# A convolution and a gated product: five convolution blocks a unit become three, and six blocks for four are made on ScalarE and GpSimd

## The chip, the cores and the metric

The kernel runs on one core of one Trainium2 chip. Its engines work side by side, each on its own queue of instructions: TensorE (PE; its weight loads are shown as PEld), VectorE (DVE), ScalarE (ACT), GpSimd (POOL) and SyncE (SP), which here only issues transfers and waits. The metric is the device time of one execution in microseconds. Before the change the median of three runs is 704.99 us (704.97 to 705.65).

## The reference

Two stages. First a causal depthwise convolution along the sequence, with seven taps a head that are a softmax over the head's weights. Then a two-layer product with the function h cos(h) between the layers.

```python
B, S, D = 8, 4096, 192;  H, K = 8, 7;  Dff = 2048      # group = D // H = 24 channels share a head's taps
w = softmax(weight, axis=-1)                            # weight is [H, K]
x_pad = zeros of K - 1 rows ahead of each sequence
y[b, s, h, g] = sum over k of w[h, k] * x_pad[b, s + k, h, g]
y = y.reshape(B * S, D)                                 # 32768 tokens of 192
hh = y @ moe_w_in                                       # 192 -> 2048
out = (hh * cos(hh)) @ moe_w_out                        # 2048 -> 192, float32
```

## The kernel before

The 32768 tokens are cut into 32 units of 1024 (`U`), and each unit into two tiles of 512 (`T`); a "first" and a "second" tile is meant by that. The 192 channels are three groups `k` of 64, so that a product over the channels is three accumulating steps (`NC`).

For each tile TensorE computes eight h groups (`mm1`, L488): one group is 256 of the 2048 hidden rows, as two halves of 128 by 512 tokens, each with 64 rows of the array, six matmuls in all, into one of three PSUM buffers. ScalarE takes the cosine of a group as a sine with a shifted phase (L510), and VectorE multiplies it with h into `g` (L514). The product with `moe_w_out` (`mm2_step`, L523) runs for the tile before: 64 steps a tile, each a pair of matmuls on the two row halves, 192 columns wide, into two banks. When a tile's 64 steps are done ("p"), the two banks are copied out (`evac`, L567), bank 0 by ScalarE (order letter `P`) and bank 1 by VectorE (`Q`), and stored (`store`).

The convolution reaches the first product as `cT`, channels on the partitions and tokens along the row, twice: once on the lower 64 partitions and once, shifted by one block, on the upper 64. From unit 4 on (`FIRST_RAW`) it is computed in two ways, and a unit is split between them:

- The first `NPB` = 5 blocks of `OP` = 112 tokens go over TensorE. GpSimd casts x to bf16 in the order of channels (`cast_unit`, L207, order letter `K`); `conv_unit` (L269, letters `c1`, `c2`) multiplies with a banded matrix of the taps, in two pieces of four matmul pairs, 16 matmuls a unit; ScalarE copies the result to `ct_buf` (L294, `ec1`, `ec2`); two DMA transposes bring it to `cT` (`turn_unit`, L309, letters `X` and `x`).
- The last `NRB` = 4 blocks of `OR` = 116 tokens stay off TensorE. One DMA transpose turns the cast x ("raw") into `rT`, channels on the partitions (`turn_raw`, L343, letter `T`). ScalarE multiplies three of the seven taps (`taps`, L352, L356; six instructions of half the width each, letters such as `a211`), GpSimd multiplies the other four in one instruction (L363) and sums up (L370, L374, L377; `conv_raw`, letter `R`), and four DMAs write the result `ro` into `cT` (`spread_raw`, L379, L387; letter `U`).

x is loaded three DMAs a unit (`load_unit`, L98, letter `L`).

Every engine's order is written out by hand. `PE_ORDER` and `ACT_ORDER` (L589, L590) have one string for the first and one for the second tile: `h0` to `h7` are the h groups, `m12` is twelve steps of mm2, a letter with a number (`K+3`) is the work above for the unit that lies so many units ahead, `O` a store. `ACT_ORDER` gives the order in which cosines (`s0` to `s7`, with VectorE's product behind each), taps and evacuations are issued. SyncE's queue takes transfers in the order in which TensorE's string names them. It also carries marks: in the middle of each tile (`q`), and between the two convolution pieces, SyncE waits for TensorE's last matmul on one set of row halves, and TensorE waits for SyncE before it writes the same bank from the other halves (class `Turn`, L191).

## Time and profile before

| | |
|---|---|
| median of the runs | 704.99 us (704.97 to 705.65) |
| span of the profiled execution | 703.5 us |
| the profiled execution's own time beside its span | not listed; the median lies 1.5 us over the span |
| TensorE busy | 697.0 us, 99% |
| VectorE busy | 642.4 us, 91% |
| ScalarE busy | 644.4 us, 92% |
| GpSimd busy | 503.7 us, 72% |
| DMA engines | mean 142 GB/s |
| granted TensorE clock | 0.999 |

The span is the time from the first to the last instruction of one execution on the profiler. In a list of groups, a row has the source line, the engine, the operation, what is written and read, the shape, the count, and then the busy time in us, the mean of one in ns, and the idle time of the engine just before these instructions with what ended it. A row of the chain of work is a start and a duration in us and what the end of the program hung on in that time. A row of windows has, for one stretch, the busy time of PE, PEld, DVE, ACT and POOL (with counts), then the clock, the busy share of the DMA engines and GB/s. A row of waits has the waiting instruction, whom it waited for, us in total, the number of times and the longest. A row of the timeline has start, duration, engine, line, operation and count; equal neighbours are merged, so that the first start and the whole duration stand there. SPq is SyncE's queue: the duration is that of the issuing, and the landing of a transfer is counted from the start of its issue.

### The profile page before, as it was taken

To read this page: it belongs to the slowest core of one execution; us is meant where nothing else is said; L and a number is where in the kernel's file an instruction comes from. 1 tells how busy PE (TensorE), PEld (TensorE's weight loads), DVE (VectorE), ACT (ScalarE), POOL (GpSimd) and SP (SyncE) were. 2 spreads that over 40 slices of the span, in tenths; PEclk is the share of its full clock that TensorE was granted. 3 is DMA by queue.
4 is the path that set the end of the run, shared out by engine and by line. 5 is a ranking of instruction groups with operands and counts; after the bars stand their busy time and mean duration, and the time that the engine had idled before them with its cause. 6 is when DMAs were issued, how large, how long until landed. Compare 5 with 4: busy or idle time off the path is not lost.

```text
span 703.5 us, 26826 instructions
## 1 busy us (share of the span) xinstructions
PE 697.0 (99%) x11830; PEld 512.8 (73%) x11830; DVE 642.4 (91%) x598; ACT 644.4 (92%) x831; POOL 503.7 (72%) x214
## 2 busy tenths in 40 slices
PE   8999999999999999999999999999999999999997
PEld 4677777777777777777777777777777777777776
DVE  6889999999999999999999999999999999999996
ACT  7889999999999999999999999999999999999875
POOL 6524478977778877778877688877789778799400
PEclk9999999999999999999999999999999999999999
DMA  8964456667667768676656577577665576874331
GB/s 214 234 167 97 120 135 143 138 147 164 138 153 146 131 145 176 134 152 131 147 152 153 150 159 129 140 161 150 143 147 132 145 174 137 153 127 95 92 91 47
DMA packets 228292, 100.09 MB, mean 142 GB/s; under 512 B 156240, under 2 KB 227792, under 8 KB 228176
## 3 DMA queue, kind: packets, MB, share of 16 engines
q1 hardware_dynamic: 227464, 97.40, 62.7%
q8 instruction: 92, 1.51, 0.9%
q0 software_dynamic: 416, 0.79, 0.7%
q14 instruction: 24, 0.20, 0.1%
q10 hardware_dynamic: 296, 0.20, 0.1%
HBM read 31.36 MB, written 25.17 MB: 80 GB/s over the span
## 4 chain that ended last, share of the span: by engine, by line
PE 96%; DMA 1%; DVE 1%; POOL 0%; SPq 0%; ACT 0%; issue 0%; POOLq 0%
PE o_ps L552 48%; PE h L503 46%; PE h L277 2%; DMA wo_f<-in_moe_w_out_dram 1%; PE h L552 0%; SPq L124 0%; PE h L229 0%; DVE band L415 0%; POOL wo L120 0%; POOL mask L159 0%; DVE ct L438 0%; PE o_ps L432 0%; ACT mask L164 0%; DVE diag L404 0%; DVE prod L401 0%
## 5 line engine op out<-in xcount | busy, mean ns | idle before, releaser
L514 DVE TENSOR_TENSOR g<-h,cs 128x1024 bf16<-128x1024 f32 (+1 forms) x513 | 604.9, 1216 | 27.9 <-ACT cs L510 24.5
L510 ACT ACTIVATE cs<-h 128x1024 bf16<-128x1024 f32 (+1 forms) x513 | 511.0, 1021 | 44.0 <-PE h L503 30.6
L552 PEld LDWEIGHTS <-g 64*128 64x128 bf16 x8192 | 354.2, 94 | 102.2 <-issue 1.0
L552 PE MATMUL o_ps<-wo,g 64*128 64x192 bf16 x8128 | 420.6, 243 | 0.1
L503 PE MATMUL h<-cT,w 64*128 64x512 bf16 (+1 forms) x3078 | 407.0, 376 | 0.8 <-DVE g L514 0.4
L503 PEld LDWEIGHTS <-w 64*128 64x128 bf16 x3078 | 147.6, 94 | 75.0 <-issue 1.8
L211 POOL CAST xk<-x_f 128x768 bf16<-128x768 f32 (+1 forms) x56 | 76.4, 1367 | 113.9 <-DMA x_f<-in_x_dram 109.3
L363 POOL TENSOR_TENSOR raw_prod<-rT,tap 128x2784 f32<-128x2784 bf16 x28 | 135.3, 4832 | 0.2
L370 POOL TENSOR_TENSOR raw_prod<-raw_prod,pa 128x2088 f32<-128x2088 f32 x28 | 129.1, 4609 | 2.2
L356 ACT ACTIVATE pa<-rT,tap 128x348 f32<-128x348 bf16 x168 | 94.6, 580 | 0.0
L374 POOL TENSOR_TENSOR raw_prod<-raw_prod 128x1392 f32<-128x1392 f32 x28 | 87.9, 3138 | 2.2
L571 DVE COPY o_sb<-o_ps 128x384 f32<-128x384 f32 x62 | 34.6, 557 | 23.7 <-PE o_ps L552 23.5
L377 POOL TENSOR_TENSOR ro<-raw_prod 128x696 bf16<-128x696 f32 x28 | 46.5, 1660 | 2.2
L294 ACT CAST ct_buf<-h 112x480 bf16<-112x480 f32 x56 | 28.6, 562 | 4.1 <-PE h L277 0.6
L571 ACT COPY o_sb<-o_ps 128x384 f32<-128x384 f32 x64 | 30.8, 482 | 0.1
L277 PE MATMUL h<-xk,band 64*112 64x120 bf16 x448 | 21.2, 213 | 0.0
L277 PEld LDWEIGHTS <-band 64*112 64x112 bf16 x448 | 18.0, 127 | 0.0
L219 POOL CAST x_bf<-x_f 128x768 bf16<-128x768 f32 (+2 forms) x5 | 9.1, 1812 | 7.0 <-DMA x_f<-in_x_dram 6.9
L307 POOL COPY ct<-ct 128x1728 bf16<-128x1728 bf16 x3 | 4.9, 1630 | 8.9 <-ACT ct L239 8.9
L394 POOL COPY cT<-cT 128x144 bf16<-128x144 bf16 x3 | 0.9, 308 | 13.5 <-DMA cT<-ct 13.5
L136 PE MATMUL o_ps<-zero 128*128 128x512 bf16 x21 | 7.2, 492 | 1.3 <-DVE zero L131 1.3
L239 ACT CAST ct<-h 128x432 bf16<-128x432 f32 x12 | 5.9, 530 | 0.4 <-issue 0.4
(66 smaller groups left out, 52.7 us busy)
## 6 DMA issues: line engine op xcount, KB each, us to landing
out_dram<-o_sb SPq DMA_DIRECT2D x63, 384.0 KB, 3.7
x_f<-in_x_dram SPq DMA_DIRECT2D x28, 480.0 KB, 5.5
x_f<-in_x_dram SPq DMA_DIRECT2D x56, 192.0 KB, 2.7
cT<-ro SPq DMA_DIRECT2D x112, 87.0 KB, 2.3
x_f<-in_x_dram SPq DMA_DIRECT2D x4, 384.0 KB, 5.6
wo_f<-in_moe_w_out_dram SPq DMA_DIRECT2D x4, 384.0 KB, 7.9
x_f<-in_x_dram SPq DMA_DIRECT2D x2, 768.0 KB, 5.2
cT<-ct_buf SPq DMA_TRANSPOSE x56, 4.0
```

The costliest lines, as they stand in the source:

```text
L211: copy(out=xk[u][:, NC * n0 : NC * n1].rearrange("p (k n) m -> p k n m", k=NC), in_=x_tiles[u][:, n0:n1].rearrange("p n (m k) -> p k n m", ...
L277: return nc.tensor.matmul(out=ps[h // 4][0:OP, 0 : NPB * 4 * G].rearrange("p (m i r) -> p i m r", m=NC * NPB, i=4)[:, h % 4], lhsT=band[si ...
L356: mul(pa[u][:, j, part], tap_window(u, j)[:, part], tap[:, j : j + 1])
L363: nc.gpsimd.tensor_tensor(out=p, in0=tap_window(u, PA, K), in1=tap[:, PA:K].rearrange("p (j a b) -> p j a b", a=1, b=1).to_broadcast([128, ...
L370: add(out=p[:, 0:m], in0=p[:, 0:m], in1=a[:, done : done + m], op=ALU.add)
L374: add(out=p[:, 0:m], in0=p[:, 0:m], in1=p[:, n - m : n], op=ALU.add)
L377: add(out=ro[u], in0=p[:, 0], in1=p[:, 1], op=ALU.add)
L503: nc.tensor.matmul(out=h[:, i, n0 * 128 : n1 * 128], lhsT=w[rows, k, j, :], rhs=rhs, start=(k == 0), stop=(k == NC - 1))
L510: nc.scalar.activation(out=cs[:, :, part], in_=h[:, :, part], func=AF.Sin, bias=math.pi / 2.0, scale=1.0)
L514: nc.vector.tensor_tensor(out=g_tiles[t][:, 2 * j : 2 * j + 2, part], in0=h[:, :, part], in1=cs[:, :, part], op=ALU.mult)
L552: ms.append(nc.tensor.matmul(out=o_ps[tt, b, si], lhsT=g_tiles[tt][rows, f, s * 128 : (s + 1) * 128], rhs=wo[rows, f // 2, f % 2, :], star ...
L571: (copy or copies[b])(o_sb[t][:, 2 * b : 2 * b + 2, :].rearrange("p s d -> p (s d)"), o_ps.pop((t, b)))
```

## The change

From unit 4 on:

- Three blocks of 112 tokens a unit go over TensorE, and six of 115 beside it. They overlap by `OVER` = 2 tokens, which the spread leaves out. The convolution matmuls have 72 columns for 120, and their weights 128 columns for 112 (the rows beyond 112 are written but not read).
- ScalarE makes three taps, each in a left part of five and a right part of four of the nine rows of `rT` (575 and 460 elements). They are written with a shift of six elements in their buffer.
- GpSimd makes the other four taps with one instruction each (`tap_raw`, letter `R`), and the three sums in a step of their own (`sum_raw`, letter `S`).
- In the first tile VectorE copies out bank 0 as well (letter `V` in place of `P`).
- The orders are written anew: `R+2`, `S+2` and `U+1` in the second tile (it was `R+1` and `U+0` in the first), `X+1` and `x+1` both in the first tile, `T+3` behind `U+1`.
- `rT` has two buffers for three, and the float32 copy of `moe_w_out` uses a buffer of `g` instead of one of its own.

```diff
@@ -45,16 +45,18 @@
     FIRST_RAW = 4
-    NPB, OP = 5, 112
-    NRB = 4
-    OR = (U - NPB * OP) // NRB
+    NPB, OP = 3, 112
+    NRB = 6
+    OR = -(-(U - NPB * OP) // NRB)
+    OVER = NRB * OR - (U - NPB * OP)
     WN = NC * NRB // 2
     PA = 3
-    HALF = WN // 2
-    CW = 2 * NPB * OP
+    SHIFT = 6
+    SLOTS = 10
+    CW = SLOTS * OP
     xf = x.rearrange("b s d -> (b s) d")
@@ -65,7 +67,7 @@
     cT_pool = ctx.enter_context(tc.tile_pool(name="cT", bufs=2))
     xk_pool = ctx.enter_context(tc.tile_pool(name="xk", bufs=2))
     ro_pool = ctx.enter_context(tc.tile_pool(name="ro", bufs=2))
-    rT_pool = ctx.enter_context(tc.tile_pool(name="rT", bufs=3))
+    rT_pool = ctx.enter_context(tc.tile_pool(name="rT", bufs=2))
     pa_pool = ctx.enter_context(tc.tile_pool(name="pa", bufs=2))
     cos_pool = ctx.enter_context(tc.tile_pool(name="cos", bufs=3))
     gpool = ctx.enter_context(tc.tile_pool(name="g", bufs=3))
@@ -91,11 +93,12 @@
         if u >= FIRST_RAW:
             x_tiles[u] = xin.tile([128, UB + 1, D], FP32, name="x_f")
-            raw = NPB * OP + OR - 128
-            for n0, n1, t0, step in ((NPB, NPB + 2, raw, 2 * OR), (NPB + 2, UB + 1, raw + OR, 2 * OR), (0, NPB, OP - 128, OP)):
+            raw, half = NPB * OP - OVER + OR - 128, NRB // 2
+            for slots, t0, step in ((slice(NPB, UB + 1, 2), raw, OR), (slice(NPB + 1, UB + 1, 2), raw + half * OR, OR),
+                                    (slice(0, NPB), OP - 128, OP)):
                 rows = xf[u * U + t0 : u * U + t0 + 128, :]
-                rows = bass.AP(rows.tensor, rows.offset, [[D, 128], [step * D, n1 - n0], [1, D]])
-                queue.dma_start(out=x_tiles[u][:, n0:n1, :], in_=rows)
+                rows = bass.AP(rows.tensor, rows.offset, [[D, 128], [step * D, half if slots.step else NPB], [1, D]])
+                queue.dma_start(out=x_tiles[u][:, slots, :], in_=rows)
             return
         if n0 == 0:
             x_tiles[u] = xin.tile([128, UB + 1, D], FP32, name="x_f")
@@ -112,7 +115,7 @@
         nc.gpsimd.dma_start(out=w[64 * t : 64 * t + 64].rearrange("p k j f -> p k (j f)"), in_=w_src[t])
     load_unit(0, 0, NB)
-    wo_f = consts.tile([128, NP, 2, D], FP32)
+    wo_f = gpool.tile([128, NF * T // 2], FP32, name="g")[:, 0 : NP * 2 * D].rearrange("p (j i d) -> p j i d", j=NP, i=2)
     wo_src = moe_w_out.rearrange("(i j p) d -> p j i d", i=2, p=128)
     def cast_wo(q):
@@ -170,7 +173,7 @@
     nc.gpsimd.affine_select(out=ident, in_=ident, compare_op=ALU.not_equal, fill=1.0, base=0, pattern=[[1, 128]],
                             channel_multiplier=-1)
     wn = consts.tile([128, HQ, K], BF16)
-    ct_bufs = [consts.tile([128, 2 * NC * NPB + 1, 64], BF16, name="ct_buf%d" % i) for i in range(2)]
+    ct_bufs = [consts.tile([128, NC * SLOTS + 1, 64], BF16, name="ct_buf%d" % i) for i in range(2)]
     wmax = consts.tile([128, HQ, 1], FP32)
     nc.vector.tensor_reduce(out=wmax[:, :, 0], in_=w_bc, axis=mybir.AxisListType.X, op=ALU.max)
@@ -275,8 +278,8 @@
         def mm(h, side):
             first, last = h % 4 == 0 and h // 4 == side, h % 4 == 3 and h // 4 != side
             return nc.tensor.matmul(
-                out=ps[h // 4][0:OP, 0 : NPB * 4 * G].rearrange("p (m i r) -> p i m r", m=NC * NPB, i=4)[:, h % 4],
-                lhsT=band[sides[side], h, 128 - OP : 128], rhs=xk[u][sides[side], 0 : NC * NPB, R * h : R * (h + 1)],
+                out=ps[h // 4][:, 0 : NPB * 4 * G].rearrange("p (m i r) -> p i m r", m=NC * NPB, i=4)[:, h % 4],
+                lhsT=band[sides[side], h, 128 - OP : 256 - OP], rhs=xk[u][sides[side], 0 : NC * NPB, R * h : R * (h + 1)],
                 start=first, stop=last, skip_group_check=True)
         for h in range(4):
@@ -291,7 +294,7 @@
         yield
         for b in range(2):
             w0 = 4 * R * b
-            nc.scalar.copy(ct_bufs[u % 2][0:OP, 0 : 2 * NC * NPB].rearrange("p (k n) m -> p k n m", k=NC)[:, :, 1 : NPB + 1, w0 : w0 + 4 * R],
+            nc.scalar.copy(ct_bufs[u % 2][0:OP, 0 : NC * SLOTS].rearrange("p (k n) m -> p k n m", k=NC)[:, :, 1 : NPB + 1, w0 : w0 + 4 * R],
                            ps[b][0:OP, 0 : NPB * 4 * G].rearrange("p (k n w) -> p k n w", k=NC, w=4 * R))
             if b:
                 have.update((("conv", u, 0), ("conv", u, 1)))
@@ -315,7 +318,7 @@
                 have.update((("whole", u, 0), ("whole", u, 1)))
             to = cT[u][:, 0 : NC * CW].rearrange("p (n s t) -> p s n t", s=2, t=OP)
             nc.sync.dma_start_transpose(out=to[:, part],
-                                        in_=ct_bufs[u % 2][0:OP, part : part + 2 * NC * NPB].rearrange("p s m -> p (s m)"))
+                                        in_=ct_bufs[u % 2][0:OP, part : part + NC * SLOTS].rearrange("p s m -> p (s m)"))
             cT.pop(u - 2, None)
             return
         assert ("double", u) in have
@@ -349,30 +352,31 @@
         w = rT[u][:, :, t0 : t0 + OR]
         return w if j1 is None else bass.AP(w.tensor, w.offset, [w.ap[0], [1, j1 - j0], *w.ap[1:]])
-    def taps(u, j, half, mul):
+    PARTS = {"w": slice(0, WN), "l": slice(0, (WN + 1) // 2), "r": slice((WN + 1) // 2, WN)}
+    def taps(u, j, part):
         if u not in pa:
-            pa[u] = pa_pool.tile([128, PA, WN, OR], FP32, name="pa")
-        part = slice(HALF * half, HALF * (half + 1))
-        mul(pa[u][:, j, part], tap_window(u, j)[:, part], tap[:, j : j + 1])
-    raw_prod = consts.tile([128, K - PA, WN, OR], FP32)
-    def conv_raw(u):
-        a, p = pa.pop(u), raw_prod
-        nc.gpsimd.tensor_tensor(out=p, in0=tap_window(u, PA, K),
-                                in1=tap[:, PA:K].rearrange("p (j a b) -> p j a b", a=1, b=1).to_broadcast([128, K - PA, WN, OR]),
-                                op=ALU.mult)
-        add = nc.gpsimd.tensor_tensor
-        n, done = K - PA, 0
-        while done < PA:
-            m = min(n, PA - done)
-            add(out=p[:, 0:m], in0=p[:, 0:m], in1=a[:, done : done + m], op=ALU.add)
-            done += m
-        while n > 2:
-            m = n // 2
-            add(out=p[:, 0:m], in0=p[:, 0:m], in1=p[:, n - m : n], op=ALU.add)
-            n -= m
+            room = pa_pool.tile([128, 16 * (-(-(SHIFT + PA * WN * OR) // 16))], FP32, name="pa")
+            pa[u] = room[:, SHIFT : SHIFT + PA * WN * OR].rearrange("p (j w t) -> p j w t", j=PA, w=WN)
+        have.add(("tap", u, j, part.start))
+        nc.scalar.mul(pa[u][:, j, part], tap_window(u, j)[:, part], tap[:, j : j + 1])
+    NG = K - PA
+    raw_prod = consts.tile([128, NG, WN, OR], FP32)
+    def tap_raw(u):
+        p = raw_prod
+        for j in range(NG):
+            nc.gpsimd.tensor_scalar(out=p[:, j], in0=tap_window(u, PA + j), scalar1=tap[:, PA + j : PA + j + 1],
+                                    scalar2=1.0, op0=ALU.mult, op1=ALU.mult)
+    def sum_raw(u):
+        assert {("tap", u, j, PARTS[k].start) for j in range(PA) for k in "lr"} <= have
+        a, p, add = pa.pop(u), raw_prod, nc.gpsimd.tensor_tensor
+        add(out=p[:, 0:PA], in0=p[:, 0:PA], in1=a, op=ALU.add)
+        add(out=p[:, 0:2], in0=p[:, 0:2], in1=p[:, 2:4], op=ALU.add)
         ro[u] = ro_pool.tile([128, WN, OR], BF16, name="ro")
         add(out=ro[u], in0=p[:, 0], in1=p[:, 1], op=ALU.add)
@@ -380,11 +384,13 @@
         have.add(("raw", u))
         r = ro.pop(u).rearrange("p (k w) t -> p k (w t)", k=NC)
+        run = NRB // 2 * OR
         for to, t0 in ((0, NPB * OP + OP), (1, NPB * OP)):
-            d = cT[u][64 * to : 64 * to + 64, t0 : t0 + (NC - 1) * CW + NRB * OR]
-            d = bass.AP(d.tensor, d.offset, [d.ap[0], [CW, NC], [2 * OR, 2], [1, 2 * OR]])
             for v in range(2):
-                nc.sync.dma_start(out=d[:, :, v], in_=r[64 * v : 64 * v + 64])
+                skip = 0 if v else OVER
+                d = cT[u][64 * to : 64 * to + 64, t0 : t0 + (NC - 1) * CW + 2 * run - OVER]
+                d = bass.AP(d.tensor, d.offset + v * (run - OVER), [d.ap[0], [CW, NC], [1, run - skip]])
+                nc.sync.dma_start(out=d, in_=r[64 * v : 64 * v + 64, :, skip:])
     def mend_edges(u):
@@ -488,7 +494,7 @@
     def mm1(t, j, n0=0, n1=NB):
         assert ("whole", t // TPU, t % TPU) in have
-        assert t < TPU * FIRST_RAW or t % TPU == 0 or ("raw", t // TPU) in have
+        assert t < TPU * FIRST_RAW or ("raw", t // TPU) in have
         c = cT[t // TPU]
         h = h_pool.tile([128, 2, T], FP32, name="h")
         for k in range(NC):
@@ -586,15 +592,15 @@
-    PE_ORDER = ['m12 h0 m4 h1 K+3 R+1 m5 h2 m7 q h3 U+0 m6 h4 m17 h5 X+1 m9 p h6 h7 O m4', 'm11 h0 m4 h1 m6 h2 m7 q x+1 h3 m5 h4 m7 c1 m8 c2 m3 h5 T+3 L+4 m9 p O h6 h7 m4']
-    ACT_ORDER = ['s0 s1 a211 s2 s3 s4 a014 a114 Q s5 P s6 s7 a007', 's0 s1 s2 a102 s3 a203 s4 Q ec2 ec1 s5 P s6 s7']
+    PE_ORDER = ['m10 h0 m4 h1 m9 h2 m5 X+1 q h3 m1 K+3 m5 h4 m17 h5 O m9 p x+1 h6 h7 m4', 'm10 h0 m7 h1 m5 h2 R+2 m6 q h3 S+2 m8 h4 m6 c1 m12 c2 U+1 h5 T+3 O m6 L+4 p h6 h7 m4']
+    ACT_ORDER = ['s0 s1 a0l1 s2 s3 a2r3 s4 Q a1l4 V s5 a1r5 s6 s7 a0r7', 's0 s1 s2 s3 a2l3 s4 ec1 Q ec2 s5 P s6 s7']
     PE_FIRST = ["K1 h0a h0b W0 h1 h2 h3 r h4 w5 d11 w4 h5 d21 W1 c11 X0 m1 h6 m11 h7 L2 c21 D1",
                 "m6 K2 h0 m1 L3 h1 K3 m13 q h2 m3 h3 m9 h4 m6 h5 m3 X1 c12 m11 p c22 h6 d12 h7 L4 L5 m17 c13 m4 c23 m1 d22 Y1 D2 m1",
                 "h0 m2 h1 m7 q K4 h2 m11 h3 X2 O m8 h4 Y2 m13 p h5 h6 m9 h7 m7",
                 "h0 m8 h1 m8 q h2 m7 h3 m7 O m1 h4 m3 d13 m4 d23 m6 h5 m4 p T4 h6 h7 m4 D3 Z0 Z1",
                 'm12 h0 m4 h1 K+3 m5 h2 m7 q h3 m6 h4 m17 h5 X+1 m9 p h6 h7 O m4',
-                'm11 h0 m4 h1 m6 h2 m7 q x+1 Y3 h3 m5 h4 m7 c1 m8 c2 m3 h5 T+3 L+4 m9 p O h6 h7 m4']
+                'm11 h0 m4 h1 R+2 m6 h2 m7 q Y3 h3 S+2 m5 h4 m7 c1 m8 c2 m3 h5 T+3 L+4 m9 p O h6 h7 m4']
     ACT_FIRST = ["s0a s0b s1 s2 er s3 s4 ed11 ed21 s5 ec11 s6 ec21 s7",
                 "s0 s1 s2 s3 s4 s5 ec12 ec22 Q P s6 ed12 s7 ed22 ec13 ec23",
                 "s0 s1 s2 s3 Q s4 P s5 s6 s7",
@@ -629,16 +635,16 @@
                 if k[0] == "e":
                     need = k[1:] if k[1:] in conv else k[1] + "2" + k[3:]
                 else:
-                    need = "p" if k in "PQA" else "h" + k[3:] if k[0] in "ab" else "h" + (k[1:2] if k[2:] in "lr" else k[1:])
+                    need = "p" if k in "PQAV" else "h" + k[3:] if k[0] == "a" else "h" + (k[1:2] if k[2:] in "lr" else k[1:])
                 if need not in done:
                     return
                 act.pop(0)
-                if k in "PQA":
+                if k in "PQAV":
                     if 0 <= made < NT - 1:
-                        evac(made, int(k != "P"), nc.scalar.copy if k == "A" else None)
-                elif k[0] in "ab":
+                        evac(made, int(k in "QA"), {"A": nc.scalar.copy, "V": nc.vector.tensor_copy}.get(k))
+                elif k[0] == "a":
                     if u + 2 in rT:
-                        taps(u + 2, int(k[1]), int(k[2]), nc.scalar.mul if k[0] == "a" else nc.vector.tensor_scalar_mul)
+                        taps(u + 2, int(k[1]), PARTS[k[2]])
                 elif k[0] == "e":
                     next(conv[part_of(k[1:])], None)
                 elif k[0] == "s" and t < NT:
@@ -657,7 +663,7 @@
                 if v < FIRST_RAW:
                     load_edges(v)
             else:
-                {"K": cast_unit, "D": double_unit, "X": turn_unit, "Y": mend_edges, "T": turn_raw, "R": conv_raw,
+                {"K": cast_unit, "D": double_unit, "X": turn_unit, "Y": mend_edges, "T": turn_raw, "R": tap_raw, "S": sum_raw,
                  "U": spread_raw, "x": lambda u: turn_unit(u, part=1)}[k](v)
         for k in pe.split():
@@ -686,7 +692,7 @@
             elif k[1:] and k[1] != "+":
                 of_unit(k[0], int(k[1]))
             else:
-                if u + int(k[2:]) < NU and (k[0] not in "RUx" or u + int(k[2:]) >= FIRST_RAW):
+                if u + int(k[2:]) < NU and (k[0] not in "RSUx" or u + int(k[2:]) >= FIRST_RAW):
                     of_unit(k[0], u + int(k[2:]))
             done.add(k)
             flush()
```

## The prediction

> **What bounds the kernel now.** I read the page's busy shares first, then one steady unit in the view of windows, then the chain over that unit, then the waits.
>
> ```profile
> span 703.5 us, 26826 instructions
> ...
> PE 697.0 (99%) x11830; PEld 512.8 (73%) x11830; DVE 642.4 (91%) x598; ACT 644.4 (92%) x831; POOL 503.7 (72%) x214
> ```
>
> ```profile
> 296.37:317.71 21.34, 21.34 (x373) 15.65 (x371) 19.86 (x19) 20.11 (x26) 16.61 (x7) 1.00 0.70 147
> ```
>
> ```profile
> 296.37 1.40 PE o_ps L552 x34
> 297.77 0.65 PE h L503 x6
> ...
> 307.32 0.21 PE h L277 x8
> ...
> 308.19 0.21 PE h L277 x8
> ```
>
> TensorE is busy in all 21.34 us of a unit (1024 tokens, two tiles), at full granted clock, and the chain inside that unit stays on it from end to end. The unit can be added up from the chain: sixteen h groups of 0.65 us (10.4), 128 pairs of mm2 steps at 1.40/17 = 0.0824 us (10.54), and two convolution pieces of 0.21 us (0.42), together 21.36. So there is no idle time to win; a unit gets shorter only by less TensorE work, and stays shorter only if nobody else needs more than the new period. VectorE (19.86) and ScalarE (20.11) have a good microsecond left, GpSimd (16.61) over four.
>
> ```profile
> POOL xk L211 <- DMA x_f<-in_x_dram: 109.3, 47, 9.6
> ACT cs L510 <- PE h L503: 30.6, 54, 1.1
> ```
>
> The longest waits are GpSimd's for the x load and ScalarE's for TensorE; both are spare time of engines that are not the bound.
>
> **TensorE: blocks from five to three.** Removed: 8 of the 20 columns per head and k in each of the 16 convolution matmuls of a unit (120 columns become 72), in 28 units. The weights widen from 112 to 128 columns.
>
> ```profile
> L277 PE MATMUL h<-xk,band 64*112 64x120 bf16 x448 | 21.2, 213 | 0.0
> L277 PEld LDWEIGHTS <-band 64*112 64x112 bf16 x448 | 18.0, 127 | 0.0
> ```
>
> ```profile
> L552 PEld LDWEIGHTS <-g 64*128 64x128 bf16 x8192 | 354.2, 94 | 102.2 <-issue 1.0
> ```
>
> ```profile
> 13.92 0.85 PE L465 MATMUL o_ps<-x_bf,band 128*128 128x96 bf16 x16
> ```
>
> ```profile
> L465 PE MATMUL o_ps<-x_bf,band 128*128 128x96 bf16 x16 | 0.9, 207 | 0.0
> ```
>
> A piece is four pairs (two row halves run together) in 0.21 us: 0.0525 us a pair at 120 columns. An mm2 pair is 0.0824 at 192. The slope between them is 0.0299/72 = 0.415 ns a column, so 72 columns should take 0.0525 - 48 x 0.000415 = 0.0326. The 16 matmuls at L465 have new weights each and 96 columns: (0.85 - 0.207)/15 = 0.043 us apart, on the same line, so the weight load does not floor the interval there. Bounds: a pair at 0.0326, or no gain at 0.0525; a loss I exclude, since 128-column loads show 94 ns and the 112-column ones 127. I take 0.0326: 8 x 0.020 = 0.16 us a unit, 28 x 0.16 = 4.5 us, and the new period is 21.18.
>
> The Trainium skill, "TensorE: Matmul & The Clock Gate", section Back-to-back issue gap, speaks against this: in a stream of weight loads and matmuls it gives about 81 ns a matmul at 128 columns, set by both operations. By it a narrower matmul would buy nothing and the sum would stay at 705.0; the 43 ns at L465 disagree with it.
>
> **GpSimd: other instructions, more of them.** Removed: one product of four taps and three sums over 696 elements a tap. Added: four single-tap products of 1035 elements (9 x 115) from one input, and sums over 3105, 2070 and 1035. The two casts of x cover the same 1728 elements, only split 6 to 3.
>
> ```profile
> L363 POOL TENSOR_TENSOR raw_prod<-rT,tap 128x2784 f32<-128x2784 bf16 x28 | 135.3, 4832 | 0.2
> L370 POOL TENSOR_TENSOR raw_prod<-raw_prod,pa 128x2088 f32<-128x2088 f32 x28 | 129.1, 4609 | 2.2
> ...
> L374 POOL TENSOR_TENSOR raw_prod<-raw_prod 128x1392 f32<-128x1392 f32 x28 | 87.9, 3138 | 2.2
> L377 POOL TENSOR_TENSOR ro<-raw_prod 128x696 bf16<-128x696 f32 x28 | 46.5, 1660 | 2.2
> L211 POOL CAST xk<-x_f 128x960 bf16<-128x960 f32 x28 | 42.2, 1506 | 43.6 <-DMA x_f<-in_x_dram 38.9 <-ACT pa L356 4.4 <-ACT cs L510 0.3
> ...
> L211 POOL CAST xk<-x_f 128x768 bf16<-128x768 f32 x28 | 34.4, 1228 | 70.4 <-DMA x_f<-in_x_dram 70.4
> ...
> L307 POOL COPY ct<-ct 128x1728 bf16<-128x1728 bf16 x3 | 4.9, 1630 | 8.9 <-ACT ct L239 8.9
> ```
>
> Sums: (4609 - 3138)/696 = 2.11 ns an element, so 6.76 + 4.57 + 2.38 = 13.71 us. Casts 2.73. Three gaps of 2.2/28 = 0.08 before the sums: 0.24. That is 16.7 without the products. No row shows a one-input product with a scalar from a table on GpSimd. From below, the one-input bf16 copy: 1630 x 1035/1728 = 0.98 us. From above, the same product in its two-input form, 4832 x 1035/2784 = 1.80; dropping an input should not make it slower. I take 1.0, the copy, because it too reads one dense bf16 stream; 1.8 stays for a rival. GpSimd then needs 16.7 + 4.0 = 20.7 of 21.18: under the period, with almost all its slack gone. From 1.11 us a product on it is the bound.
>
> The Trainium skill, "GPSIMD Engine Reference", section 4.1, calls one-input work roughly line-rate, which by its clock would be an estimate of 0.86 us and leave the sum as it is; no run here shows this operation.
>
> The order holds: the sums wait for the last tap, asked for behind the fourth cosine of the second tile, and their result is spread one unit later, behind the convolution of the second tile. By the orders' own lengths (0.65 an h group, 0.0824 a step, a cosine and a tap behind the fourth h) the sums may start 17.2 us into a unit, take 13.9 with their gaps, and so end 9.9 us into the next, where the spread is issued at 17.3: 7.4 us to spare. The wait for x (109.3 us) is covered by the sums now.
>
> **ScalarE and VectorE.**
>
> ```profile
> L510 ACT ACTIVATE cs<-h 128x1024 bf16<-128x1024 f32 x511 | 509.9, 1023 | 43.7 <-PE h L503 30.3 <-DVE g L514 0.6
> ...
> L356 ACT ACTIVATE pa<-rT,tap 128x348 f32<-128x348 bf16 x168 | 94.6, 580 | 0.0
> ```
>
> ```profile
> L571 DVE COPY o_sb<-o_ps 128x384 f32<-128x384 f32 x62 | 34.6, 557 | 23.7 <-PE o_ps L552 23.5
> L571 ACT COPY o_sb<-o_ps 128x384 f32<-128x384 f32 x64 | 30.8, 482 | 0.1
> L294 ACT CAST ct_buf<-h 112x480 bf16<-112x480 f32 x56 | 28.6, 562 | 4.1 <-PE h L277 0.6
> ```
>
> The copies give (562 - 482)/96 = 0.83 ns an element. Six taps of 348 (3.48 us) become three of 575 and three of 460: 0.77 and 0.67 by that slope (4.32), or 0.96 and 0.77 if all of the 580 ns grew in proportion (5.17). Taken: the slope, +0.84, end +1.69. The two convolution copies go from 480 to 288 elements, -0.32; one evacuation leaves, -0.48. ScalarE comes to 20.15 (end 21.0) and VectorE to 19.86 + 0.56 = 20.42, both under 21.18. Where the moved evacuation lands has its own rows, the end of a first tile:
>
> ```profile
> 319.59 0.91 PE L552 MATMUL o_ps<-wo,g 64*128 64x192 bf16 x18
> ...
> 320.33 1.46 PE L503 MATMUL h<-cT,w 64*128 64x512 bf16 x12
> 320.53 0.56 DVE L571 COPY o_sb<-o_ps 128x384 f32<-128x384 f32 x1 [0.28 <-PE o_ps L552]
> 320.72 0.47 ACT L571 COPY o_sb<-o_ps 128x384 f32<-128x384 f32 x1
> 321.01 3.59 DVE L514 TENSOR_TENSOR g<-h,cs 128x1024 bf16<-128x1024 f32 x3
> ...
> 321.63 1.40 PE L552 MATMUL o_ps<-wo,g 64*128 64x192 bf16 x30
> ```
>
> Today the two engines empty the banks side by side. With both on VectorE the second starts where the product starts now (321.01) and ends at 321.57; mm2 wants the banks at 321.63. It fits by 0.06 us. The three products behind it come 0.48 later: the first at 321.49 to 322.71, while the next tile's first h group, which needs its buffer, is due 14 pairs (1.15 us) behind 321.63, at 322.78. Again it fits by less than 0.1. Between nothing and 0.1 us a unit can be lost here (0 to 2.8 in all); I take 0.04, 1.1 in all.
>
> **SyncE's queue.** The spread of unit u+1 (four DMAs) moves from the first tile to a place behind the second tile's convolution, ahead of the rT transpose, the store and the three loads; each of its four carries 1.5 times the bytes in as many runs, the transpose 1152 columns for 768.
>
> ```profile
> 307.70 1.22 SPq L345 DMA_TRANSPOSE rT<-xk  x1
> 308.98 2.50 SPq L98 DMA_DIRECT2D x_f<-in_x_dram  x3
> 311.58 0.45 SPq L574 DMA_DIRECT2D out_dram<-o_sb  x1
> 316.09 2.58 SPq L387 DMA_DIRECT2D cT<-ro  x4
> ```
>
> ```profile
> L345 SPq DMA_TRANSPOSE rT<-xk x28: 1209/1212/2332, 48.8 to 627.8; - x28
> ...
> DMA to landing us min/median/max: 2.7/3.4/5.1
> ```
>
> ```profile
> L387 SPq DMA_DIRECT2D cT<-ro x112: 596/612/1620, 102.7 to 681.0; - x112
> ...
> DMA to landing us min/median/max: 2.2/2.3/4.0
> ```
>
> Counted from the end of the first convolution piece (307.53): the queue starts 0.17 later, issues the spread for 2.6 (3.9 if it grows with bytes), the transpose for 1.2 to 1.8, then 0.45 and 2.5, and is free at 6.9 (to 8.8). It must take TensorE's next mark by 8.8 (50 steps, seven h groups and the second piece, after which mm2 goes on only with that mark). The spread's third DMA, the last that the next tile's first group needs, lands at 0.17 + 1.3 + 2.3 = 3.8; that group is due at 4.7 (32 steps, three h groups, the piece). The transpose lands at 2.8 + 3.4 = 6.2 (5.5 to 7.9); ScalarE's first tap wants it at about 7.4 (two h groups, four steps and a cosine of 1.02 later). So all three are hidden at the medians, and the cover is 0.9 to 1.9 us. The two cT transposes move earlier, into the gap that the spread leaves; their readers are a unit away. rT's third buffer is dropped: its reader is a unit ahead of the next write, unless GpSimd falls behind. The g buffer lent to the early weights is free two tiles before its turn. All at nothing.
>
> **Sum.** No separate time of the profiled execution is listed: its span is 703.5 and the median of the runs 704.99, so I set 1.5 around the span. 703.5 - 4.5 + 1.1 + 1.5 = 701.6 us.
>
> **The rivals.** (1) GpSimd becomes the bound. At 1.8 us a product a unit needs 16.7 + 7.2 = 23.9, 2.7 over the period; 28 x 2.7 less the 7.4 of slack is 68 on top of the forecast, some 770 us. At 1.3 us it is 21.9, 0.7 over, 13 us, 715. For it: the only product on this engine has the high price. Against it: that product has two inputs. It decides from 1.11 us a product.
>
> (2) The two evacuations on one engine are late at the end of every first tile. The most they can cost is the 0.48 us by which the second one follows the first: 28 x 0.48 - 4.5 gives 714; from 0.16 us a unit the gain is gone. For it: covers of 0.06 us. Against it: the wait falls on work that the next three h groups can take up, and ScalarE is relieved at that place.
>
> (3) The transpose of the raw rows, now behind the spread, lands after ScalarE's first tap wants it. At the slowest landing that is 0.5 us a unit (7.9 against 7.4), more if the larger transpose lands later; passed on whole it gives 705.0 - 4.5 + 14 = 714.5. For it: 3.9 us of issuing if issue time follows bytes. Against it: the medians leave 1.2 us, and TensorE has three h buffers between itself and that cosine.
>
> (4) No change: the narrower matmul is no faster (706 with the loss at the seam), or the seam takes just what TensorE gives; 704 to 706.
>
> **How the numbers follow.** Forecast 0.57 (700 to 703.5), GpSimd 0.18, evacuations 0.09, transpose 0.05, no change 0.11, in which the rule on the weight load has 0.03. I count 0.2% (1.4 us) as what can be told from no change: faster is the forecast and a hundredth of the last case, the same the rest of that case and a hundredth of the evacuations, slower what is left. The range runs from 700.0, half a microsecond under the TensorE floor of 700.5, to 718, which takes in the second and third rivals and products of up to 1.3 us, and leaves out the dear product (about 0.14) and little else.
>
> **What would show it.** Right: the convolution pieces at 0.13 us in the chain, the period at 21.2, GpSimd's products near 1.0 us with its idle time ended by ScalarE's taps, no idle TensorE. Wrong: products above 1.11 us and TensorE waiting for the landing of cT<-ro; or TensorE's mm2 waiting for VectorE's copy, or ScalarE's taps for rT, every unit.

## The result, and the profile after

The changed kernel takes 712.21 us (711.44 to 713.18 over four runs), against 705.19 for the kernel before beside it: 1.0% slower, a ratio of 1.0100 with a 95% interval of 1.0086 to 1.0114. The forecast was 701.6, a gain.

The page of the changed kernel, its span and busy shares:

```profile
span 711.4 us, 26895 instructions
...
PE 698.8 (98%) x11828; PEld 579.2 (81%) x11830; DVE 652.6 (92%) x628; ACT 642.3 (90%) x801; POOL 562.7 (79%) x298
```

Three units in the view of windows, each from the first convolution matmul of one unit to that of the next (busy us of PE, PEld, DVE, ACT, POOL, then clock, DMA share, GB/s):

```profile
245.27:266.45 21.18, 21.18 (x374) 18.29 (x371) 20.26 (x20) 20.00 (x26) 19.02 (x9) 1.00 0.77 161
331.31:353.68 22.37, 21.46 (x374) 18.64 (x371) 20.25 (x20) 20.05 (x26) 19.09 (x9) 1.00 0.72 152
374.90:396.84 21.94, 21.66 (x375) 18.08 (x371) 20.10 (x20) 20.14 (x26) 19.26 (x10) 1.00 0.71 156
```

The first is the unit that was forecast: 21.18 us, TensorE busy in all of it, the other three engines at 19.0 to 20.3. The others are 1.2 and 0.8 us longer with the same work in them. So nothing is too slow on average; in some units something is late. The waits name it:

```profile
POOL raw_prod L378 <- ACT pa L362: 69.6, 28, 4.9
...
PE h L509 <- DMA cT<-ro: 4.8, 8, 0.9
ACT pa L362 <- DMA rT<-xk: 4.1, 6, 0.8
```

The first row is GpSimd's spare time. The second is TensorE waiting for the spread, the third ScalarE's tap waiting for the transposed raw rows. Neither pair is among the waits of before. The chain of the second unit above shows the first of them:

```profile
333.19 0.04 issue
333.24 4.16 DMA cT<-ro
337.40 0.04 issue
337.44 0.69 PE h L509 x5
```

In SyncE's queue the same spread and the transpose behind it, and the row of the spread over the run (duration of an issue: least, median, most):

```profile
331.93 3.93 SPq L393 DMA_DIRECT2D cT<-ro  x4
335.96 1.34 SPq L348 DMA_TRANSPOSE rT<-xk  x1
```

```profile
L393 SPq DMA_DIRECT2D cT<-ro x112: 598/615/1978, 94.3 to 677.3; - x112
...
DMA to landing us min/median/max: 2.6/2.9/4.6
```

The third of the units above (375 to 397) waits for the transpose. These are rows of its timeline: first ScalarE's first tap, then VectorE behind it with the two evacuations, then the last h group of the first tile and mm2 on TensorE:

```profile
383.49 0.79 ACT L362 ACTIVATE pa<-rT,tap 128x575 f32<-128x575 bf16 x1 [0.78 <-DMA rT<-xk]
```

```profile
385.21 3.62 DVE L520 TENSOR_TENSOR g<-h,cs 128x1024 bf16<-128x1024 f32 x3 [1.10 <-ACT cs L516]
388.74 1.01 DVE L577 COPY o_sb<-o_ps 128x384 f32<-128x384 f32 x2
```

```profile
388.88 0.82 PE L509 MATMUL h<-cT,w 64*128 64x512 bf16 x6 [0.18 <-DVE g L520]
389.81 1.33 PE L558 MATMUL o_ps<-wo,g 64*128 64x192 bf16 x28
```

A tap 0.78 us late puts 1.10 us of idle time into VectorE, whose products and copies then end behind the time at which TensorE's last h group and the next mm2 steps want them (389.75 for the copies, 389.81 for mm2).

The whole loss is found by setting the last matmul of every h group, counted from the start of its unit, against that of a clear unit. The 26 units between 93.8 and 655.5 us take 11.04 us more than 26 x 21.18. Of that, 7.7 us arise at the first h group of a unit (the spread), 3.35 between the sixth group of a first tile and the first of the second (the transpose); no other place loses. Which units lose follows a pattern of eight. The position is that of the unit's first convolution matmul in TensorE's list of instructions, modulo 256, and us over 21.18 are given for each of the 26 units, in order of time:

```
position   159       127             95            63              31             255           223           191
at spread  0 0 0 0   .15 .76 .10 0   .35 .60 .29   1.12 1.19 1.25  .66 .04 1.00   .04 .02 .03   0 .02 .02     .05 .03 .04
at end     0 0 0 0   0 0 0 0         0 0 0         0 0 0           0 0 0          .19 .66 .69   .71 .58 .52   0 0 0
```

### The profile page after: what moved, and what is told of

Same layout as the page of the kernel before. It is cut to its first block, busy times and chain, and to the rows that moved or that the text cites. A ratio compares the mean times of both kernels' runs of the same rounds, so it can differ in the third digit from the quotient of the medians.

```text
span 711.4 us, 26895 instructions
## 1 busy us (share of the span) xinstructions
PE 698.8 (98%) x11828; PEld 579.2 (81%) x11830; DVE 652.6 (92%) x628; ACT 642.3 (90%) x801; POOL 562.7 (79%) x298
## 4 chain that ended last, share of the span: by engine, by line
PE 86%; DMA 6%; SPq 3%; DVE 2%; ACT 2%; issue 1%; POOL 0%; POOLq 0%; ACTq 0%
PE h L509 43%; PE o_ps L558 42%; DMA cT<-ro 5%; SPq L393 3%; ACT cs L516 1%; PE h L280 1%; DVE o_sb L577 1%; DMA rT<-xk 1%; DVE g L520 0%; PE h L558 0%; PE h L232 0%; DVE band L421 0%; ACT ct L478 0%; POOL mask L162 0%; ACT pa L362 0%
## 5 line engine op out<-in xcount | busy, mean ns | idle before, releaser
L558 PEld LDWEIGHTS <-g 64*128 64x128 bf16 x8192 | 406.0, 94 | 59.1 <-issue 6.3
L509 PE MATMUL h<-cT,w 64*128 64x512 bf16 (+1 forms) x3078 | 443.1, 376 | 6.3 <-DMA cT<-ro 4.8
L558 PE MATMUL o_ps<-wo,g 64*128 64x192 bf16 x8128 | 447.4, 243 | 0.5
L509 PEld LDWEIGHTS <-w 64*128 64x128 bf16 x3078 | 203.3, 94 | 59.3 <-issue 12.0
L378 POOL TENSOR_TENSOR raw_prod<-raw_prod,pa 128x3105 f32<-128x3105 f32 x28 | 159.0, 5680 | 69.6 <-ACT pa L362 69.6
L362 ACT ACTIVATE pa<-rT,tap 128x575 f32<-128x575 bf16 (+1 forms) x168 | 122.8, 731 | 4.1 <-DMA rT<-xk 4.1
L371 POOL TENSOR_SCALAR raw_prod<-rT,tap 128x1035 f32<-128x1035 bf16 x112 | 126.2, 1149 | 0.1
L379 POOL TENSOR_TENSOR raw_prod<-raw_prod 128x2070 f32<-128x2070 f32 x28 | 107.8, 3852 | 2.2
L214 POOL CAST xk<-x_f 128x1152 bf16<-128x1152 f32 (+1 forms) x56 | 75.3, 1377 | 0.8 <-DMA x_f<-in_x_dram 0.8
L381 POOL TENSOR_TENSOR ro<-raw_prod 128x1035 bf16<-128x1035 f32 x28 | 66.8, 2385 | 2.2
```

What stands on the lines that cost most here:

```text
L214: copy(out=xk[u][:, NC * n0 : NC * n1].rearrange("p (k n) m -> p k n m", k=NC), in_=x_tiles[u][:, n0:n1].rearrange("p n (m k) -> p k n m", ...
L362: nc.scalar.mul(pa[u][:, j, part], tap_window(u, j)[:, part], tap[:, j : j + 1])
L371: nc.gpsimd.tensor_scalar(out=p[:, j], in0=tap_window(u, PA + j), scalar1=tap[:, PA + j : PA + j + 1], scalar2=1.0, op0=ALU.mult, op1=ALU. ...
L378: add(out=p[:, 0:PA], in0=p[:, 0:PA], in1=a, op=ALU.add)
L379: add(out=p[:, 0:2], in0=p[:, 0:2], in1=p[:, 2:4], op=ALU.add)
L381: add(out=ro[u], in0=p[:, 0], in1=p[:, 1], op=ALU.add)
```

## Experiments

The theories: S, the late spread holds up TensorE's first h group; T, the late transpose holds up ScalarE's first tap; V, the two evacuations on VectorE are late by themselves; F, what makes a transfer late in some units is an instruction fetch of TensorE on the same DMA engines.

**The spread's order.** The line numbers of the changed kernel apply.

```diff
-        for to, t0 in ((0, NPB * OP + OP), (1, NPB * OP)):
-            for v in range(2):
+        for v in range(2):
+            for to, t0 in ((0, NPB * OP + OP), (1, NPB * OP)):
```

> The four transfers of the spread are only issued in another order: the two that the first tile reads go first, the two that only the second tile reads go last; same place, same bytes. Theory S (the time was lost because TensorE's first h group waits for the spread's third transfer, which lands 4.9 to 6.2 us behind the start of the first convolution piece while the group is due at about 4.9): the last transfer that this group needs is now the second, landing at about 4.1 to 5.3, so of the some 7.7 us that the h groups at the start of a unit lost, about 7 come back: 705, with the units that lose time at the end of the first tile unchanged. Theory V (the evacuations on VectorE are late) and theory T (the raw transpose is late for ScalarE) expect no change: 712.

708.39 us (ratio to before 1.0040, 1.0025 to 1.0055): 3.8 of the 7 us came back. Unit by unit the loss at the first h group falls from 7.7 to some 2 us, as S says. The rest is T's, which grew; its row of the waits:

```profile
ACT pa L362 <- DMA rT<-xk: 5.7, 8, 1.0
```

The loss at the spread that is left lies in six units. With less time lost there, TensorE reaches the tap's place earlier; eight units now lose 0.05 to 0.9 us at the end of the first tile, 4.7 in all. I had counted T's part as fixed, and that was the miss.

**The spread early.**

```diff
-... h4 m17 h5 O m9 p x+1 h6 h7 m4'
+... h4 x+1 m17 h5 O m9 p h6 h7 m4'
-'m10 h0 m7 h1 ... c1 m12 c2 U+1 h5 T+3 ...
+'m10 h0 U+1 m7 h1 ... c1 m12 c2 h5 T+3 ...
```

> The spread goes from behind the second convolution piece to behind the second tile's first h group, some 6 us earlier, and the second cT transpose from the end of the first tile to behind its fifth h group so that the spread does not wait for it. The raw transpose then has no spread ahead of it in the queue. Theory S with T (both late transfers come from the spread's new place): nearly all units at 21.18 us, 700.5 to 702.5. Theory V: the units that lose 0.5 to 0.7 us at the end of the first tile stay, 704 to 705. If marks in the queue then come late for TensorE, a new wait at the middle of the second tile or at the second convolution piece, up to 0.5 us a unit, 710.

701.44 us (701.38 to 701.55), ratio 0.9948, 0.9933 to 0.9963. Every one of the 26 units takes 21.18 us, with no wait of TensorE for cT<-ro and none of a tap for rT. The unit in windows, and its two convolution pieces in the chain:

```profile
305.50:326.68 21.18, 21.18 (x375) 16.33 (x371) 20.18 (x20) 20.05 (x27) 18.99 (x9) 1.00 0.76 161
```

```profile
305.63 0.13 PE h L280 x8
...
306.75 0.13 PE h L280 x8
```

The long issues are still there, only nothing waits for them:

```profile
L393 SPq DMA_DIRECT2D cT<-ro x112: 595/612/2081, 87.3 to 662.9; - x112
```

S and T together hold all of the loss, and V none: both evacuations are still on VectorE. This version is faster than either kernel, by 3.7 us against before.

**The transpose first.**

```diff
-... c2 U+1 h5 T+3 O ...
+... c2 T+3 U+1 h5 O ...
```

> The raw transpose goes ahead of the spread instead of behind it. Theory T: no unit loses time at the end of the first tile any more (about 3.3 us back). Theory S: the spread starts 1.3 to 1.4 us later and every unit's first h group waits that long, 27 x 1.3 = 35 us, less the 3.3: about 740 to 745. If the first h group did not hang on the spread, 709.

762.14 us (1.0815, 1.0798 to 1.0832). The direction is S's; the size was short by 20 us. No unit loses time at the end of the first tile any more, as T says. In the nine units that lose least the loss is 1.5 to 1.6 us: the third transfer of the spread is issued some 3.3 us behind the first convolution matmul, where the changed kernel's clear units have 1.9, and takes 3.1 to 3.2 us to land. 26 such units would be 40 us. The other 20 lie in the 17 units that lose 1.8 to 4.6, four of them also at the second and third h groups; in most of them the issue of the transpose or of the spread is lengthened, up to 2.2 and 1.6 us, or a landing is. I had priced only the transpose's issue. TensorE's row of the waits:

```profile
PE h L509 <- DMA cT<-ro: 41.1, 40, 1.5
```

**The evacuation back on ScalarE.**

```diff
-'s0 s1 a0l1 s2 s3 a2r3 s4 Q a1l4 V s5 a1r5 s6 s7 a0r7'
+'s0 s1 a0l1 s2 s3 a2r3 s4 Q a1l4 P s5 a1r5 s6 s7 a0r7'
```

> The evacuation of bank 0 in the first tile goes back to ScalarE. Theory V: the some 3.3 us lost at the end of first tiles come back, 709. Theory T: what is late there is the raw transpose, then ScalarE's tap, then the cosines; the time stays at 712 within a microsecond, or gets longer, since ScalarE has 0.48 us more to do in the late units.

737.44 us (1.0453, 1.0436 to 1.0471): 25 us slower than the changed kernel. V had forecast a gain, and T at most a loss without a size. Its clear units take 22.12 us. The reason stands in ScalarE's timeline, at the end of a first tile:

```profile
331.44 0.79 ACT L362 ACTIVATE pa<-rT,tap 128x575 f32<-128x575 bf16 x1
332.95 0.48 ACT L577 COPY o_sb<-o_ps 128x384 f32<-128x384 f32 x1 [0.72 <-PE o_ps L558]
333.33 1.03 ACT L516 ACTIVATE cs<-h 128x1024 bf16<-128x1024 f32 x1
```

The copy has to wait 0.72 us for mm2 to end, and the sixth cosine stands behind it in the queue. In the changed kernel VectorE does that waiting and ScalarE goes on.

**The evacuation behind the cosine.** On the version with the early spread:

```diff
-... s4 Q a1l4 V s5 a1r5 ...
+... s4 Q a1l4 s5 P a1r5 ...
```

> The version with the early spread, and the first tile's bank 0 again copied out by ScalarE, but behind its sixth cosine, where it stood before the change, not ahead of it. Putting it back ahead of that cosine had cost 25 us: ScalarE stood idle 0.72 us in front of the copy each unit, waiting for mm2 to end, with the cosine behind it. If that wait is all: the cosine fills it, ScalarE has 0.48 us more of 21.18, and the time is 701 to 704. If ScalarE simply has no 0.48 us to spare beside the longer taps: 0.2 to 0.9 us a unit, 707 to 727.

706.94 us (1.0025, 1.0015 to 1.0035): between the two expectations. Units take 21.37, 0.19 over the floor, without the 0.72 us wait. So most of the 0.94 us was the wait in front of the cosine; the remainder goes with the copy on ScalarE, and I did not take it apart further. One of the units in windows:

```profile
222.40:243.77 21.37, 21.37 (x374) 16.37 (x370) 19.90 (x19) 20.32 (x27) 19.01 (x9) 1.00 0.77 160
```

**The tap later.** On the version with the other order of the spread:

```diff
-'s0 s1 a0l1 s2 s3 ...
+'s0 s1 s2 a0l2 s3 ...
```

> The version with the spread's transfers in the other order, and ScalarE's first tap one cosine later in its order (about 1.3 us), so that it need not wait for the raw transpose. Theory T: in that version 8 units lost 0.5 to 0.9 us at the end of the first tile, 4.7 us in all, each with a wait of a tap for rT; they come back, 703.5 to 705, the late second transfer staying with about 2 us. If those losses have another cause (the two evacuations on VectorE): 708 still.

709.63 us (1.0069, 1.0052 to 1.0086), slower where a gain was expected, and yet T holds: no tap waits for rT any more, and no unit loses 0.5 to 0.9 us at the end of the first tile. But every unit now takes 21.43 or more, as this one in windows, and no transfer is late in most of them. The 0.25 us arise each time at the first h group of the second tile; that the tap crowds the cosines behind it is my reading, not shown apart:

```profile
223.00:244.43 21.43, 21.36 (x373) 16.33 (x370) 20.18 (x20) 20.09 (x27) 19.02 (x9) 1.00 0.74 159
```

26 x 0.25 = 6.5 us given, some 4.7 taken back, and 0.9 at the spread, where 1.1 of 2.0 are left.

**The phase of the fetches, clear and hit.** The 92 packets of the queue of kind "instruction", 16 KB each, stand beside 23,659 TensorE instructions, 257 to a packet; a unit has 736 of these, which is 2.875 x 256, and so the pattern of eight.

```profile
q8 instruction: 92, 1.51, 0.9%
```

In the late unit of 331 us one of them falls on the spread; this is the row of the view of DMA for 333.2 to 335.3 us, where the four issues take 3.93 us (the rows of SyncE's queue above) and not four times the median of 0.615:

```profile
q8 instruction: 1, 0.02, 4.5%
```

The times of the packets in the trace give their place in every unit, counted from its first convolution matmul. At the positions 127 to 63 one starts 0.8 to 2.0 us into the unit, and the issue of the spread under way at that time (the second or the third) takes 0.9 to 2.0 us. At 31 one starts at 3.0 to 4.2, before the third transfer lands at 4.9. At 191 the first comes at 6.0 or later, and at 159, but for one unit, at 8 or later, when the spread has landed.

To fix the phase, sixteen matmuls a unit are split, which makes 768 instructions; the two kernels differ only in the tile from which this is done (8 and 14). The split restarts the accumulation for half of the tokens, so these two kernels leave out a part of the first product; the work is otherwise that of the changed kernel. The line of the first product is L514 here.

```diff
+                if t >= 8 and k == 0 and i == 0 and n1 - n0 == NB:
+                    for c0 in (0, T // 2):
+                        nc.tensor.matmul(out=h[:, i, c0 : c0 + T // 2], lhsT=w[rows, k, j, :], rhs=rhs[:, c0 : c0 + T // 2],
+                                         start=True, stop=False, skip_group_check=True)
+                    continue
...
```

> Theory F: the spread's issue is lengthened, and its landing late, in the units in which one of TensorE's instruction fetches (16 KB packets, 92 in the run; 92 x 256 = 23,552 of its 23,659 instructions, so 256 instructions a fetch) falls upon it. A unit has 736 TensorE instructions, 2.875 fetches, so the place drifts and comes round every 8 units, as the late units do. Here sixteen matmuls of 512 columns a unit are split into two of 256, which makes 768 instructions, just three fetches, so that the place stays fixed from unit 6 on: at position 153 of 256 for the first convolution matmul, a place near which the changed kernel lost 0.05 us. The order of everything else is the changed kernel's. F expects nearly every unit without loss: 702 to 706, the splits costing 0.05 to 0.15 us a unit. Without F (the late units come from something else): 712 plus the splits, 713 to 716.

> The same splits, begun three units later, so that the place stays fixed at position 57 of 256, near which the changed kernel lost 1.2 to 1.3 us a unit. F expects that loss in each of the 23 units behind: 23 x 1.2 = 28 us over the other phase, 728 to 736. Without F: the same time as the other phase within 2 us.

705.22 us (704.79 to 705.57) with the clear phase, 724.68 (723.95 to 725.70) with the other. The same program but for its phase differs by 19.5 us; F holds, at some 0.9 us a unit rather than 1.2. In the phase that hits, TensorE waits for the spread in nearly every unit (the row of the waits, and the row of the spread's issues with its landings):

```profile
PE h L514 <- DMA cT<-ro: 16.1, 26, 1.0
```

```profile
L393 SPq DMA_DIRECT2D cT<-ro x112: 596/612/2137, 94.2 to 689.5; - x112
...
DMA to landing us min/median/max: 2.7/3.7/4.3
```

In the clear one it hardly does:

```profile
PE h L514 <- DMA cT<-ro: 0.9, 4, 0.3
```

```profile
L393 SPq DMA_DIRECT2D cT<-ro x112: 595/615/1638, 94.3 to 669.3; - x112
...
DMA to landing us min/median/max: 2.7/2.9/3.8
```

From 350 us on its units take 21.2 each. Before that, some still lose up to 0.55 us, 2.6 in all, with the spread's second issue lengthened to 0.65 to 1.43 us. The trace shows where this ends: up to there a packet starts 0.6 to 1.4 us into each unit, and from there on, in nearly all, at some 21 us, just ahead of the next unit. Why it moves is open.

The packets go with TensorE's instructions: these two kernels have 24,556 and 24,460 of them, and 96 and 95 packets. In neither does a tap wait for rT, which speaks for a late transpose that hangs on the phase too. How a packet makes it late is less clear than for the spread: at the positions 255 and 223, where it was late, one starts 5.0 to 6.4 us into the unit, but at 191, where it was not, one starts at 6.0 to 6.5.

The Trainium skill, "Runtime: NRT & Kernel Launch", section Terms, says that each engine's instruction memory is refilled in blocks of 16 KiB. The trace agrees (92 packets of 16,384 bytes), and the two phases show what such a refill costs a transfer beside it.

**The width of the weights.** On the version with the early spread:

```diff
-                out=ps[h // 4][:, 0 : NPB * 4 * G]...
-                lhsT=band[sides[side], h, 128 - OP : 256 - OP], ...
+                out=ps[h // 4][0:OP, 0 : NPB * 4 * G]...
+                lhsT=band[sides[side], h, 128 - OP : 128], ...
```

> The version with the early spread, its convolution weights back at 112 columns (the moving side stays at 72). If the pace of the narrow pairs is set by the moving columns alone: 21.18 us a unit and 701.4 as with 128. If the slower 112-column load (127 ns against 95) sets it, up to 0.02 us a pair come back: 21.34 a unit, 706.

704.63 us (0.9995, 0.9985 to 1.0004): 3.2 of the 3.7 us are gone. The chain has the pieces at 0.19 and the unit takes 21.30:

```profile
307.03 0.19 PE h L280 x8
```

```profile
306.85:328.15 21.30, 21.30 (x374) 16.40 (x371) 20.18 (x20) 20.06 (x27) 19.00 (x9) 1.00 0.75 160
```

A pair takes 0.19/4 = 0.048 us with 112 weight columns and 0.033 with 128. A load takes 128 ns with 112 columns and 95 with 128. So the weight columns do set the pace, and the time lies between my two expectations; that it is the load through which they do is argued, not shown apart.

**Without the shift.** On the version with the early spread:

```diff
-    SHIFT = 6
+    SHIFT = 0
```

> The version with the early spread, ScalarE's taps written without the shift of six elements. GpSimd's first sum took 5.68 us for 3105 elements where the rows of before gave 6.76. If the shift (24 bytes between the two inputs' places modulo 64, as also between the inputs of the second sum, 8280 bytes apart) is what makes it fast: the first sum at about 6.7 us, the second unchanged at 3.85, GpSimd 20.4 us a unit and its wait for the taps shorter by 1.1, the time unchanged at 701.4 since that is still under 21.18. If not: 5.7 us as with the shift.

701.70 us (0.9950, 0.9933 to 0.9968), the same as with the shift (701.44) within the spread of the runs, and the first sum as expected for an effect of the shift (from the list of groups):

```profile
L378 POOL TENSOR_TENSOR raw_prod<-raw_prod,pa 128x3105 f32<-128x3105 f32 x28 | 189.8, 6777 | 30.2 <-ACT pa L362 30.2
...
L379 POOL TENSOR_TENSOR raw_prod<-raw_prod 128x2070 f32<-128x2070 f32 x28 | 107.8, 3848 | 2.2
```

6.78 us against 5.68 with the shift, the second sum unchanged. The wait for the taps falls by the difference, from 60.1 us in the version with the early spread to 30.2 (28 x 1.1 = 31).

## Why the prediction was wrong

**TensorE: right.** The pieces came out at 0.13 us, the period at 21.18 and, with the spread early, the time at 701.44 against 701.6. That it came so near is in part luck: the span fell by 3.9 us (703.5 to 699.6), not by the 4.5 of the sum, and the 1.1 us for the seam, which were not lost, more than made up for that. The rival by which a narrower matmul buys nothing did not come: a pair went from 0.0525 to 0.033. What I had not seen is how the gain hangs on the 128 weight columns: at 112 the pair takes 0.048, not 0.033.

**GpSimd: not the bound, as forecast, but by two errors that pull against each other.** Its groups in the changed kernel:

```profile
L378 POOL TENSOR_TENSOR raw_prod<-raw_prod,pa 128x3105 f32<-128x3105 f32 x28 | 159.0, 5680 | 69.6 <-ACT pa L362 69.6
L371 POOL TENSOR_SCALAR raw_prod<-rT,tap 128x1035 f32<-128x1035 bf16 x112 | 126.2, 1149 | 0.1
L379 POOL TENSOR_TENSOR raw_prod<-raw_prod 128x2070 f32<-128x2070 f32 x28 | 107.8, 3852 | 2.2
L381 POOL TENSOR_TENSOR ro<-raw_prod 128x1035 bf16<-128x1035 f32 x28 | 66.8, 2385 | 2.2
```

The product takes 1.15 us, not 1.0, and past the 1.11 that I named as the point where GpSimd binds: 16.7 + 4.6 would be 21.3. But the first two sums take 9.53 us where I had 11.33, and GpSimd stays at 19.0 (20.7 forecast), waiting 2.5 us a unit for the taps. I had priced the sums by the rows of before; the first is faster by the shift of six elements, which the change has and the sum did not reckon with. The first rival did not come, though not for my reason.

**ScalarE and VectorE: right.** The taps take 777 and 686 ns (770 and 670 taken). The seam on VectorE that I gave 0 to 0.1 us a unit, and the rival on it 0.09, cost nothing in a clear unit: in that from 245.27 the two copies end at 259.34, and mm2 wants the banks at 259.65, a cover of 0.3 us where I had 0.06.

**SyncE's queue: here it failed.** "The spread's third DMA [...] lands at 0.17 + 1.3 + 2.3 = 3.8; that group is due at 4.7": the cover of 0.9 us does not exist. The landing of 2.3 us was that of transfers of 87 KB; at 129 KB it is 2.9 in the median. In clear units the third transfer is issued 1.9 us behind the first convolution matmul and lands at 4.9, just when the group starts, which is where I had it (4.7 behind the end of the piece). I had the landing at 3.9 on that count: 0.7 of the missing microsecond is the landing of 3.0 in place of 2.3, and 0.3 is the issue, 1.9 behind the first matmul in place of 1.6. And the issues were taken at their median. Of the row "596/612/1620" I used the 612 and made nothing of the 1620. A transfer that is due every unit meets the long issue in a fixed share of the units, here about four in eight, whatever the median says. I had no cause for the long issues and did not look for one; the 92 instruction packets stood on the page of the profile.

The step "All at nothing" should have read: no cover left at the medians, and 0.1 to 1.2 us lost where an issue is long. Four such units in eight, 0.6 us each on average (the table's positions 127 to 31), is 28 x 0.3 = 8 us, and the sum, 701.6 + 8, comes out slower than before.

The third rival, the late transpose, is there as a mechanism, at 0.05 and a price of 14 us; it took 3.35, in six units, in which the first tap starts 8.1 to 8.6 us into the unit and not at 7.6. That TensorE waits for the spread itself was only named among the signs of a wrong forecast, under GpSimd's lateness, and had no chance of its own.

## What to carry to other kernels

A transfer moved closer to its reader is to be costed with its own bytes and with the long end of the issue and landing times, not the median: in a kernel whose bound engine never rests, every late unit is lost for good, and units that come early give nothing back. Here the whole difference between 712 and 701 us is the place of the spread's four transfers in one queue, with one cT transpose moved to make room. And where an engine's order has an instruction that must wait, ask what stands behind it: the same copy cost 0.94 us a unit ahead of a cosine and 0.19 behind it.

## What the runs showed of the hardware

- TensorE's own instruction fetches, one 16 KB packet to some 256 instructions, lengthen the issue and the landing of transfers on which they fall: an issue of 0.6 us becomes up to 2.1, a median landing of 2.9 us 3.7. A loop with 736 instructions a turn meets them in a pattern of eight turns; with 768 the phase stays. Between two phases of one program lay 19.5 us of 705.
- GpSimd adds two float32 streams at (5680 - 196)/3105 = 1.77 ns an element when ScalarE's taps are written six elements (24 bytes) into their buffer, and at (6777 - 196)/3105 = 2.12 when they are not (196 ns is what the sums of before leave at no elements). The second sum, whose inputs are 8280 bytes apart, 24 modulo 64, takes 1.77 with and without the shift. The third, 4140 bytes apart (44 modulo 64), takes (2385 - 196)/1035 = 2.11, and the second and third sums of before (0 and 32 modulo 64) take 2.11 and 2.10. That the distance modulo 64 is what counts fits all of these, if the two buffers of the first sum both begin on a multiple of 64 bytes; no run shows that, or other distances.
- A pair of matmuls of 72 columns on two row halves takes 0.033 us with 128 weight columns and 0.048 with 112.
